# Block 3's state projection by Strassen's scheme among the output products, the residual seeded into Z, and one sum of block 0 and two S4 sums by DMA

## The chip, the cores and the metric

One core of a Trainium2 chip. The metric is device time in microseconds (us), the median of several executions. The traces below are of one execution each; a trace's span is about 2 us shorter than the time. A ratio is the mean time of one kernel's fast runs over that of the other's of the same rounds on the same chip, so it is not quite the ratio of the medians that are quoted.

Names used below: PE is TensorE's matmuls (PEld its weight loads), DVE is VectorE, ACT is ScalarE, POOL is GpSimd, SP is SyncE, which here only issues DMAs. PSUM is the memory in which matmuls leave their results; to evacuate it is to copy them out. An accumulating DMA adds what it carries to what stands at its destination; its landing is the moment at which the transfer is complete. PEq and SPq in the views are the sequencers of PE and SP. "L504" is line 504 of the kernel that ran, so one statement has different numbers in different kernels.

## The reference

The input is x of shape (1, 2048, 512). It is layer-normalised, and three things are added: x itself, a diagonal state-space model, and a gated MLP.

```python
xn = _layernorm(x)                                  # (x - mean) / sqrt(var + 1e-5)
# state-space part, complex, 512 states
Bu   = einsum("bld,pd->blp", xn, B_bar)             # "state projection": re and im parts
h_t  = Lam_bar * h_{t-1} + Bu_t                     # a scan over 2048 steps
y    = 2 * einsum("blp,dp->bld", h, Cmat).real + xn * Dskip
# gated MLP, 1792 hidden units
out2 = (silu(xn @ w1) * (xn @ w3)) @ w2
return x + y + out2                                 # bfloat16
```

## The kernel before

The 2048 rows are cut into four blocks (0 to 3) of 512. Each block has these stages: the MLP's first two products ("gate stage", `glu`), the state projection (`bu`), a chain of VectorE and DMA steps around the scan (`ssm_tasks`), and the output products (`y_fast`). Rows of the output are done in eight pairs of 128-row tiles: pairs 0 and 1 belong to block 0, pairs 2 and 3 to block 1, pairs 4 and 5 to block 2, pairs 6 and 7 to block 3. Each pair is a 2 x 2 block product by the Winograd form of Strassen's scheme: seven products instead of eight, for sums of the factors (S1 to S4 of the left one, T1 to T4 of the right one). The gate stage of block 3 uses the same scheme (`glu_last`), so the kernel already knows how.

The order of TensorE's work in the second half is: gate stage of block 2, projection of block 3, pairs 2 and 3, gate stage of block 3, pairs 4 to 7.

VectorE's work is queued in a list (`bg`, class `Filler`) and taken out while TensorE works, with an estimate of both engines' clocks. All of it is fixed when the kernel is built; in the traces a piece of VectorE's work keeps its place in that order even when its operands are ready sooner (in e3, below, a 0.4 us addition with its operand ready at 176.6 us started at 183.14, behind 6 us of other work).

```python
class Filler:                                    # shortened
    def fill(self, lead=None):                   # emit queued work while the VectorE clock is behind
        limit = self.pe + (self.lead if lead is None else lead)
        while self.tasks and self.dve + 0.5 * self.tasks[0][0] <= limit:
            if not getattr(self.tasks[0][1], "ready", lambda: True)():
                return
            self.pop()
    def flush(self, key):                        # emit everything up to the last task with this key
        last = max((i for i, t in enumerate(self.tasks) if t[2] == key), default=-1)
        for _ in range(last + 1):
            self.pop()
```

```python
def bu(b):                                       # state projection: 32 matmuls of 512 columns
    for hf in range(NPT // 2):
        u = up.tile([P, 2, 2, TBLK], BF16, name="u")
        for j in range(2):
            for ri in range(2):
                ...
                for dt in range(NDT):
                    nc.tensor.matmul(out=ps, lhsT=bt[:, ri, dt, ...], rhs=xnT_blk[b][:, dt, :], ...)
                nc.scalar.activation(out=u[:, j, ri, :], in_=ps, func=ACT.Copy)

def ssm_tasks(b, posts_last=False, between=(), middle=(), late=()):
    def half(hf):                                # two halves of the states
        def pre_c():                             # u += p : on VectorE for block 0 and half 0 of block 2
            if b == 0 or (b, hf) == (2, 0):
                nc.vector.tensor_tensor(out=st["g"], in0=st["g"], in1=st["p"], op=ALU.add)
            else:
                gp.dma_start(out=st["g"], in_=st["p"], accum_op=ALU.add)   # an accumulating DMA
        def scan(j, ri): ...                     # 4 scans of 1.2 us in each half
        def post_c():                            # act += p16: by accumulating DMA, but for the last half
            ...
    if b == 0:
        add(*pre0, *scans0, *post0, *pre1, *scans1, *post1)
        return
    ...

def row_sums(n, b, p):                           # S3 = a11-a21, S1 = a21+a22, S2 = a22-S3
    return [S3 on VectorE,
            S1 on VectorE if n in (0, 1, 6, 7) else S1 by accumulating DMA,
            S2 on VectorE]                       # (in words; the code is in the whole kernel)

def y_fast(n, then=()):                          # output products of pair n, shortened
    def product2():
        mms(f, v["a12"], weight(1, D1), False)
        nc.vector.tensor_tensor(out=v["s4"], in0=v["a12"], in1=v["s2"], op=ALU.subtract)   # S4
        add(o1[:, D1], f, o1[:, D1])
        if n + 1 < len(pairs) and n not in (1, 3):
            seeds(n + 1)                         # residual of the next pair into PSUM; flushes ("res", b)
    def product7():
        mms(g, v["s3"], tsum[2], False)
        add(q[2], g, o2[:, D1])                  # three PSUM additions
        add(o2[:, D2], g, q[1])
        add(o2[:, D1], z, q[2])
        store(c1 + 1, o2)
    ...
    for i in ((1, 5, 2, 6, 4, 3, 7) if b == 0 else (1, 4, 2, 6, 5, 7, 3)):
        products[i - 1]()
```

## Time and profile before

Median 203.0 us (202.85 to 203.09). What matters:

| stage | from, us | PE busy | DVE busy |
|---|---|---|---|
| start, gate stage and scan of block 0 | 0 to 50 | 49.2 of 50 | 42.9 |
| blocks 1 and 2 | 50 to 117 | 66.8 of 67 | 66.1 |
| projection of block 3, pairs 2 and 3 | 117 to 141 | 24.0 of 24 | 22.1 |
| gate stage of block 3 | 141 to 164 | 23.0 of 23 | 22.1 |
| pairs 4 and 5 | 164 to 181 | 17.0 of 17 | 15.2 |
| pairs 6 and 7 | 181 to 198 | 17.0 of 17 | 11.5 |

Five of the lines behind it, from the view of busy time by stretches of the kernel before; the first is the second part of block 0. The columns are: stretch, its length, busy time (and instructions) of PE, PEld, DVE, ACT and POOL, granted clock of TensorE as a share, mean load of the DMA engines, GB/s.

```profile
35.00:50.00 15.00, 15.00 (x71) 6.86 (x70) 14.90 (x17) 13.22 (x24) 3.62 (x4) 1.00 0.66 194
...
117.00:141.00 24.00, 24.00 (x188) 18.17 (x187) 22.06 (x30) 7.94 (x16) 6.56 (x5) 1.00 0.66 98
141.00:164.00 23.00, 23.00 (x152) 14.62 (x150) 22.07 (x32) 17.54 (x33) 0.86 (x1) 1.00 0.42 68
164.00:181.00 17.00, 17.00 (x156) 15.05 (x154) 15.24 (x24) 3.29 (x9) 2.84 (x2) 1.00 0.50 68
181.00:198.00 17.00, 17.00 (x179) 15.48 (x177) 11.46 (x23) 2.15 (x7) 0.00 (x0) 1.00 0.11 37
```

TensorE is busy all the time. A busy PE need not be a fast one, so the pace has to be read too: in the chain of waits, 8 matmuls of 512 columns take 1.73 us and 22 of 256 columns take 2.40 us, 216 and 109 ns each. These are three lines of the kernel before's chain (start, length, what):

```profile
117.72 1.73 PE bu_ps L438 x8
...
133.04 2.40 PE y_ps L865 x22
...
141.44 3.45 PE gu_ps L671 x16
...
```

From the first to the last of these, 141.44 - 117.72 = 23.72 us, TensorE did block 3's projection and pairs 2 and 3. And these are all the waits of TensorE that the waits view of the kernel before shows (engine, line, for whom: us in total, times, longest):

```profile
PE bu_ps L194 <- PEq L1049: 0.8, 1, 0.8
PE gu_ps L539 <- DMA xnT<-xn: 0.2, 1, 0.2
```

So the kernel's time is the sum of its TensorE work, a head of 5 us and a tail of 3 us. VectorE has little room: in 35 to 117 us it is busy 99% of the time.

### The profile page before, as it was taken

To read this page: it belongs to the slowest core of one execution; us is meant where nothing else is said; L and a number is where in the kernel's file an instruction comes from. 1 tells how busy PE (TensorE), PEld (TensorE's weight loads), DVE (VectorE), ACT (ScalarE), POOL (GpSimd) and SP (SyncE) were. 2 spreads that over 40 slices of the span, in tenths; PEclk is the share of its full clock that TensorE was granted. 3 is DMA by queue.
4 is the path that set the end of the run, shared out by engine and by line. 5 is a ranking of instruction groups with operands and counts; after the bars stand their busy time and mean duration, and the time that the engine had idled before them with its cause. 6 is when DMAs were issued, how large, how long until landed. Compare 5 with 4: busy or idle time off the path is not lost.

```text
span 201.1 us, 3551 instructions
## 1 busy us (share of the span) xinstructions
PE 197.2 (98%) x1353; PEld 126.4 (63%) x1353; DVE 180.4 (90%) x256; ACT 127.2 (63%) x257; POOL 47.9 (24%) x70
## 2 busy tenths in 40 slices
PE   8999999999999999999999999999999999999994
PEld 2974444444444588844444445888566678888893
DVE  4699699999999999989999989998989998988833
ACT  4799788699999967957797676110588771101110
POOL 7160289600310053043005011315100003100000
PEclk9999999999999999999999999999999999999999
DMA  5999995980582043925895955294960002951011
GB/s 160 328 248 258 290 157 170 347 216 0 105 156 55 0 91 68 177 87 106 132 157 104 97 106 108 17 156 80 163 148 0 3 0 15 113 104 52 10 62 39
DMA packets 34225, 23.56 MB, mean 117 GB/s; under 512 B 21792, under 2 KB 32160, under 8 KB 34208
## 3 DMA queue, kind: packets, MB, share of 16 engines
q0 software_dynamic: 8096, 9.84, 32.3%
q1 hardware_dynamic: 25536, 13.21, 26.6%
q10 hardware_dynamic: 576, 0.30, 0.5%
q8 instruction: 10, 0.16, 0.3%
q14 instruction: 7, 0.06, 0.1%
HBM read 7.74 MB, written 2.10 MB: 49 GB/s over the span
## 4 chain that ended last, share of the span: by engine, by line
PE 59%; DVE 33%; DMA 3%; issue 2%; POOL 1%; ACT 1%; DVEq 0%
PE gu_ps L865 13%; PE gu_ps L539 12%; PE y_ps L865 7%; PE gu_ps L671 7%; PE bu_ps L865 4%; DVE u L484 4%; DVE act L557 4%; PE y_ps L438 3%; PE bu_ps L438 3%; PE y_ps L693 3%; DMA xnT<-xn 3%; DVE tw L796 2%; PE bu_ps L194 2%; DVE u L467 2%; DVE p L463 2%
## 5 line engine op out<-in xcount | busy, mean ns | idle before, releaser
L539 PE MATMUL gu_ps<-xnT,w_sb 128*128 128x512 bf16 x312 | 68.2, 379 | 0.2 <-DMA xnT<-xn 0.2
L539 PEld LDWEIGHTS <-w_sb 128*128 128x128 bf16 x312 | 30.4, 98 | 36.8 <-DMA xnT<-xn 0.5
L865 PEld LDWEIGHTS <-act 128*128 128x128 f16 x462 | 43.5, 98 | 5.4
L549 ACT ACTIVATE u<-gu_ps 128x512 bf16<-128x512 f32 x41 | 24.8, 606 | 5.8 <-PE gu_ps L539 5.1
L548 ACT ACTIVATE g<-gu_ps 128x512 bf16<-128x512 f32 x41 | 24.7, 603 | 5.4 <-PE gu_ps L539 5.1
L438 PEld LDWEIGHTS <-bt 128*128 128x128 bf16 x128 | 12.5, 98 | 15.1
L484 DVE TENSOR_TENSOR_SCAN u<-rho,act,u 128x512 bf16<-128x512 f32 x16 | 19.8, 1269 | 0.0
L824 POOL DMA_DIRECT2D act<-act x4 | 8.0, 2002 | 33.8 <-DVE tw L820 28.9
L865 PE MATMUL gu_ps<-w_sb,act 128*128 128x256 bf16 (+3 forms) x126 | 15.9, 267 | 0.0
L671 PE MATMUL gu_ps<-xnT,w_sb 128*128 128x512 bf16 x64 | 15.9, 379 | 0.0
L438 PE MATMUL y_ps<-xnT,bt 128*128 128x512 bf16 x64 | 15.1, 379 | 0.0
L438 PE MATMUL bu_ps<-xnT,bt 128*128 128x512 bf16 x64 | 15.1, 379 | 0.0
L557 DVE TENSOR_TENSOR act<-g,u 128x1024 f16<-128x1024 bf16 x21 | 14.2, 678 | 0.6 <-ACT u L549 0.6
L501 POOL DMA_DIRECT2D act<-p x7 | 6.3, 907 | 32.2 <-DVE act L494 28.2
L683 ACT ACTIVATE g<-gu_ps 128x512 bf16<-128x512 f32 x14 | 8.4, 598 | 5.7 <-PE gu_ps L671 5.3
L440 ACT ACTIVATE u<-y_ps 128x512 bf16<-128x512 f32 x16 | 9.5, 595 | 2.3 <-PE y_ps L438 2.1
L440 ACT ACTIVATE u<-bu_ps 128x512 bf16<-128x512 f32 x16 | 9.5, 595 | 2.0 <-PE bu_ps L438 1.9
L865 PE MATMUL bu_ps<-w_sb,act 128*128 128x256 bf16 (+3 forms) x84 | 10.4, 264 | 0.0
L865 PE MATMUL gu_ps<-ct,act 128*128 128x256 f16 (+1 forms) x72 | 10.4, 267 | 0.0
L484 DVE TENSOR_TENSOR_SCAN u<-rho,ends,u 128x512 bf16<-128x512 f32 x8 | 10.0, 1271 | 0.0
L467 DVE TENSOR_TENSOR u<-u,tabe 128x2048 bf16<-128x2048 bf16 x8 | 9.8, 1220 | 0.1
L490 DVE TENSOR_TENSOR p<-u,tabe 128x2048 f16<-128x2048 bf16 x8 | 9.8, 1220 | 0.1
(163 smaller groups left out, 342.3 us busy)
## 6 DMA issues: line engine op xcount, KB each, us to landing
act<-p POOLq DMA_DIRECT2D x7, 512.0 KB, 5.2
xn<-x_blk POOLq DMA_DIRECT2D x4, 512.0 KB, 5.8
out_dram<-xn SPq DMA_DIRECT2D x15, 128.0 KB, 2.6
w_sb<-in_B_w_dram SPq DMA_DIRECT2D x1, 1792.0 KB, 8.0
w_sb<-in_B_w_dram SPq DMA_DIRECT2D x2, 768.0 KB, 5.9
u<-x_blk POOLq DMA_DIRECT2D x3, 512.0 KB, 6.5
act<-act POOLq DMA_DIRECT2D x4, 352.0 KB, 6.8
w_sb<-in_B_w_dram SPq DMA_DIRECT2D x4, 256.0 KB, 4.3
```

The costliest lines, as they stand in the source:

```text
L438: nc.tensor.matmul(out=ps, lhsT=bt[:, ri, dt, pt * P:(pt + 1) * P], rhs=xnT_blk[b][:, dt, :], start=(dt == 0), stop=(dt == NDT - 1))
L440: nc.scalar.activation(out=u[:, j, ri, :], in_=ps, func=ACT.Copy)
L467: nc.vector.tensor_tensor(out=st["g"], in0=st["g"], in1=tabe[:, psl, 0:1, :].to_broadcast(FULL), op=ALU.mult)
L484: nc.vector.tensor_tensor_scan(out=v, data0=rho[:, pt:pt + 1].to_broadcast([P, TBLK]), data1=v, initial=init, op0=ALU.mult, op1=ALU.add)
L490: nc.vector.tensor_tensor(out=st["p16"][:, :, ::-1, :], in0=st["g"], in1=tabe[:, psl, 1:3, :], op=ALU.mult)
L539: nc.tensor.matmul(out=ps[:, tsl], lhsT=w[:, dt, f * P:(f + 1) * P], rhs=xnT[:, dt, tsl], start=(dt == 0), stop=(dt == NDT - 1))
L548: nc.scalar.activation(out=g16[:, f % 2, :], in_=g_ps, func=ACT.Silu)
L549: nc.scalar.activation(out=u16[:, f % 2, :], in_=u_ps, func=ACT.Copy)
L557: nc.vector.tensor_tensor(out=act(b)[:, k0:k1 + 1:k1 - k0, :], in0=g16, in1=u16, op=ALU.mult)
L671: nc.tensor.matmul(out=ps, lhsT=w[:, dt, f * P:(f + 1) * P], rhs=xnT[:, dt, :], start=(dt == 0), stop=(dt == NDT - 1))
L683: nc.scalar.activation(out=g16[:, f % 2, :], in_=side(w1_sb, f), func=ACT.Silu)
L865: nc.tensor.matmul(out=out, lhsT=left[:, k, :], rhs=right[k][:, cols], start=(start and k == 0), stop=(k == NK - 1), skip_group_check=True)
```

## The change

The intent is to take columns off TensorE. Block 3's projection is done by Strassen's scheme too: seven products of 4 matmuls of 256 columns for each half, 56 in all, instead of 32 of 512. To give the scheme's sums and PSUM evacuations time, the seven steps are woven between the products of pairs 2 (half 0) and 3 (half 1). That costs VectorE some 5 us, which is given back elsewhere: the residual is seeded into the PSUM tile Z, so product 7 needs two PSUM additions instead of three; S4 of pairs 4 and 5 is formed by an accumulating DMA and the third product, which needs it, is put off into the next pair; and one of the sums of block 0's states goes from VectorE to an accumulating DMA.

The core of the diff (renamings, moved sums, signs and the new function's inner steps are cut):

```diff
+    LATER = (4, 5)
@@ ssm_tasks
             def pre_c():
-                if b == 0 or (b, hf) == (2, 0):
+                if (b, hf) in ((0, 0), (2, 0)):
                     nc.vector.tensor_tensor(out=st["g"], in0=st["g"], in1=st["p"], op=ALU.add)
                 else:
                     gp.dma_start(out=st["g"], in_=st["p"], accum_op=ALU.add)
@@
         if b == 0:
-            add(*pre0, *scans0, *post0, *pre1, *scans1, *post1)
+            add(*pre0, *pre1, *scans0, *post0, *scans1, *post1)
@@ new: bu_fast(b, hf), the Strassen projection of one half
+        def one():
+            product(g, a11, b11, True)
+            copy(f, g)
+            subtract(s2, s13, a11)
+        ...
+        return deque(((one, five), (two, six), (seven,), (three,), (four,)))
@@ y_fast
+        nc.scalar.activation(out=z, in_=o2[:, D1], func=ACT.Copy)     # in seeds(): residual into Z
...
-            bg.own(0.85, -1.1)
-            nc.vector.tensor_tensor(out=v["s4"], in0=v["a12"], in1=v["s2"], op=ALU.subtract)
+            if n in LATER:
+                gp.dma_start(out=v["s4"], in_=v["s2"], accum_op=ALU.add)
+            else:
+                bg.own(0.85, -1.1)
+                nc.vector.tensor_tensor(out=v["s4"], in0=v["a12"], in1=v["s2"], op=ALU.add)
...
-            mms(z, v["a22"], tsum[3], True)
+            mms(z, v["a22"], tsum[3], False)
+            copy(q[2], z)
...
-            add(q[2], g, o2[:, D1])
+            add(o2[:, D1], g, q[2])
             add(o2[:, D2], g, q[1])
-            add(o2[:, D1], z, q[2])
@@ the loop over the products
-            products[i - 1]()
+            if i == 3 and n in LATER:
+                later[n] = product3
+            else:
+                products[i - 1]()
+            if i == 5 and n - 1 in later:
+                later.pop(n - 1)()
+                if n + 1 < len(pairs):
+                    seeds(n + 1)
+            if between:
+                for step in between.popleft():
+                    step()
+                    bg.fill()
@@ the main sequence
-    bu(3)
-    posts = ssm_tasks(3, True, between=up_sums(3))
-    res_difference(3)
-    posts()
-    y_fast(2, row_sums(3, *pairs[3]))
-    bg.flush(("ssm", 2))
-    y_fast(3, row_sums(4, *pairs[4]))
+    bg.flush("cols")
+    ssm_tasks(3, middle=[(0.0, after_y2, None), *row_sums(4, *pairs[4])])
+    res_difference(3)
+    keep_ends(1)
+    y_fast(2, row_sums(3, *pairs[3]), bu_fast(3, 0))
+    y_done.append(2)
+    y_fast(3, (), bu_fast(3, 1))
```

## The prediction

> **What bounds the kernel now.** TensorE. In the table of busy time by stage, PE is busy from about 5 to 198 us but for one gap of 0.2 us near 86 (a wait for the transposed block 2); the span is 201.1 us. It also runs at full pace: in the chain of waits 8 matmuls of 512 columns take 1.73 us (216 ns each), 11 of 256 columns 1.20 us (109 ns each), and the granted clock is 1.00. [...] So time falls only if PE gets fewer columns. VectorE is a close second: 180 us busy, 96 to 99% from 25 to 118, 93% from 118 to 190 (66.6 of 72 us).
>
> **What the change removes.** Block 3's projection is 6.91 us of PE (four pieces of 1.73 in the chain). Strassen makes it 56 matmuls of 256 columns: at 109 ns, 6.1 us. Gain on PE: 0.8 us. All else on PE keeps its count.
>
> **What it adds and moves on VectorE.** New: two halves x (three sums at about 0.34 us start to start, two PSUM adds at 0.64) and two first sums, about 5.3 us. Given back: one PSUM add of 0.34 us in each of eight pairs by seeding the residual into Z (2.7), S4 of pairs 4 and 5 (2 x 0.81), one 1.14 us add of block 0 sent by DMA: about 5.4. Net near zero; the column sums only move earlier. ScalarE gains two 0.37 us copies per pair, in windows where it is 1 to 2 us busy of 8.
>
> So the critical path loses 0.8 us, if VectorE keeps its dates. That is the risk: block 3's u comes later relative to its scans (half 0 at the end of pair 2, half 1 late in pair 3), so more is left to do between 140 and 181. From start-to-start durations I get about 37 us of VectorE work in some 40 before pair 6 needs block 3's states. Today pair 6's S2 ends at 184.3, about 0.3 us before its product; the reordered S2 wins back 0.8. The accumulating DMAs of this shape landed after 6.6 to 7.7 us; S4 of pair 4 has about 9 us between issue and its deferred product, S1 of pair 5 about 7. I allow 0.2 us of PE stalls.
>
> The tail (last PE end 198.2, last VectorE add 198.5, last store to 201.1) should stay: the last adds wait for the last product's halves, not for the removed add. The head should stay too.
>
> **Predicted: 202.4 us** (203.0 - 0.8 + 0.2), 8 in 10 between 201.7 and 203.5. Faster by over 2%: 0.01; within 2%: 0.975; slower by over 2%: 0.015.
>
> **What would show it right.** PE busy without new gaps; block 3's projection as 14 products of 0.44 us among pairs 2 and 3; the last gate stage (141.3 us) starting about 0.8 us earlier; VectorE busy 180 +/- 1.5 us; the tail unchanged.
>
> **What would show it wrong.** PE gaps in pairs 2 and 3 that wait for VectorE (column sums come only just before pair 2); PE gaps in pairs 5 and 6 that wait for VectorE or an accumulating DMA; pair 4 (164.5) not starting earlier. With several such gaps the time could be 204 to 206. If freed VectorE time instead closes the gap near 86: 202.0.

"Full pace" rests on the granted clock of 1.00. 203.0 - 0.8 + 0.2 = 202.4 us, with 0.8 from the measured 216 and 109 ns (6.91 - 6.1) and 0.2 the author's estimate.

## The result, and the profile after

The changed kernel takes 207.92 us (207.55 to 208.36, 4 runs) against 203.01 us for the kernel before; the ratio is 1.0244, with a 95% interval of 1.0218 to 1.0269. It is slower by 2.4%, outside the predicted range.

First the same view of stretches, for the changed kernel. The stages begin later here, so the borders from 117 us on are moved with them (121, 144, 167, 185).

```profile
35.00:50.00 15.00, 12.20 (x58) 5.58 (x57) 10.57 (x13) 9.14 (x17) 2.79 (x4) 1.00 0.86 225
...
121.00:144.00 23.00, 23.00 (x212) 20.50 (x210) 21.31 (x34) 10.78 (x24) 3.69 (x3) 1.00 0.43 63
144.00:167.00 23.00, 22.84 (x146) 14.30 (x148) 22.24 (x28) 17.62 (x33) 3.73 (x4) 1.00 0.62 96
167.00:185.00 18.00, 16.65 (x151) 14.55 (x150) 16.03 (x21) 4.87 (x14) 6.74 (x4) 1.00 0.87 86
185.00:203.00 18.00, 17.71 (x183) 15.80 (x181) 11.74 (x22) 3.12 (x10) 0.00 (x0) 1.00 0.27 54
```

The stretch of 121 to 144 us shows the intended effect, and it is exactly as large as intended. In the chain of waits of the changed kernel these lines mark its ends:

```profile
121.27 1.20 PE gu_ps L965 x11
...
144.19 0.21 PE gu_ps L764
...
```

144.19 - 121.27 = 22.92 us for the projection and pairs 2 and 3 together, 0.80 us less than the 23.72 of before. TensorE is busy all of it. The loss lies elsewhere, and the waits of TensorE name it. All of them, for the changed kernel:

```profile
PE gu_ps L544 <- ACT g L553: 2.8, 1, 2.8
PE gu_ps L965 <- DMA act<-x_blk: 1.4, 1, 1.4
PE bu_ps L965 <- DVE act L1007: 0.9, 1, 0.9
PE bu_ps L195 <- PEq L1174: 0.8, 1, 0.8
PE gu_ps L965 <- DMA act<-p: 0.3, 1, 0.3
```

Four gaps are new: 2.8 us near 48 us, 0.9 near 79, 1.4 near 182 and 0.3 near 185. That is 5.4 us, less the 0.2 us gap of before that is gone, less the 0.8 us gained: 4.4 us of the 4.8 by which the spans differ (205.9 and 201.1).

### The gap near 48 us

The releaser that the waits view gives, ACT, is only the last link. Here is the timeline of the changed kernel around it, PE, DVE, ACT, POOL and SP mixed and lines left out (start, length, engine, line, operation, out<-in, and in brackets how long the engine was idle before it, and for whom):

```profile
31.21 0.57 SPq L182 DMA_DIRECT2D w_sb<-in_B_w_dram  x1
...
31.80 1.25 DVE L470 TENSOR_TENSOR u<-u,tabe 128x2048 bf16<-128x2048 bf16 x1
...
35.92 1.00 POOL L477 DMA_DIRECT2D u<-p  x1
...
39.78 1.21 DVE L497 TENSOR_TENSOR act<-u,tabe 128x2048 f16<-128x2048 bf16 x1
...
45.41 1.22 DVE L487 TENSOR_TENSOR_SCAN u<-rho,u 128x512 bf16<-128x512 f32 x1 [4.43 <-DMA u<-p]
46.56 0.67 DVE L562 TENSOR_TENSOR act<-g,u 128x1024 f16<-128x1024 bf16 x1
...
47.31 0.60 ACT L553 ACTIVATE g<-gu_ps 128x512 bf16<-128x512 f32 x1 [4.14 <-DVE act L562]
...
47.96 2.32 PE L544 MATMUL gu_ps<-xnT,w_sb 128*128 128x512 bf16 x10 [2.80 <-ACT g L553]
```

Read backwards. TensorE starts again at 47.96, when ACT had emptied a PSUM tile. ACT had been waiting 4.14 us for a VectorE multiplication (L562), because it needed a buffer that this multiplication frees. That multiplication stands in VectorE's queue behind a scan (L487), and the scan waited 4.43 us for the accumulating DMA `u<-p`, the block 0 sum that used to be a VectorE addition. Its data were ready at 33.05, when L470 ended; it was issued at 35.92, after GpSimd's queue had worked off a row of small operations; and it landed at 45.4. In the kernel before, the same place reads:

```profile
41.10 1.22 DVE L472 TENSOR_TENSOR u<-u,p 128x2048 bf16<-128x2048 bf16 x1
...
42.25 0.68 DVE L557 TENSOR_TENSOR act<-g,u 128x1024 f16<-128x1024 bf16 x1
...
42.85 1.22 DVE L484 TENSOR_TENSOR_SCAN u<-rho,u 128x512 bf16<-128x512 f32 x1
```

The addition (L472) takes 1.2 us, and the multiplication and the scan follow at once. The landing times of these DMAs, from the view of the source line, are first those of the changed kernel (six transfers, `u<-p` and the like; the 9.5 is block 0's) and then those of the kernel before (five; the 8.7 is one issued at 138 us, 1.1 us behind another accumulating DMA):

```profile
DMA to landing us min/median/max: 4.5/5.0/9.5
```
```profile
DMA to landing us min/median/max: 4.6/5.6/8.7
```

### The gaps near 182 and 185 us

The third product of pair 4 was put off into pair 5 to give S4's DMA time, and it still came too early. From the timeline of the changed kernel, lines left out:

```profile
170.54 1.93 POOL L920 DMA_DIRECT2D act<-act  x1 [12.25 <-DVE tw L913]
...
171.62 2.80 POOL L1004 DMA_DIRECT2D act<-x_blk  x1
...
172.94 2.42 POOL L504 DMA_DIRECT2D act<-p  x1
...
181.98 0.94 PE L965 MATMUL gu_ps<-w_sb,act 128*128 128x256 bf16 x7 [1.35 <-DMA act<-x_blk]
...
185.61 0.61 PE L965 MATMUL gu_ps<-ct,act 128*128 128x256 f16 x4 [0.29 <-DMA act<-p]
```

Three accumulating DMAs are issued within 3 us: S1 of pair 5 (L920), S4 of pair 4 (L1004) and the states of block 3's first half (L504). S4 lands 10.3 us after its issue, and the states 12.6 us. The same kind of transfer (L920 here, L824 before, 352 KB in rows of 256 bytes; the trace of the kernel before has 1424 packets for the one at 167.65 us) landed after 6.6 to 7.7 us in the kernel before, which was the basis of the prediction. Two of those four had no other accumulating DMA issued near them (6.6 us each), and two had one of 512 KB issued within 1.1 us (7.7 and 6.9 us); none had a second one of its own kind just ahead:

```profile
DMA to landing us min/median/max: 10.3/10.3/10.3
```
```profile
DMA to landing us min/median/max: 6.6/6.8/7.7
```

### The profile page after: what moved, and what is told of

Its sections match the earlier page's. It is cut to its first block, busy times and chain, and to the rows that moved or that the text cites. A ratio compares the mean times of both kernels' runs of the same rounds, so it can differ in the third digit from the quotient of the medians.

```text
span 205.9 us, 3633 instructions
## 1 busy us (share of the span) xinstructions
PE 196.4 (95%) x1365; PEld 128.3 (62%) x1377; DVE 180.3 (88%) x258; ACT 133.2 (65%) x277; POOL 50.7 (25%) x73
## 4 chain that ended last, share of the span: by engine, by line
PE 47%; DVE 22%; issue 16%; DMA 9%; POOL 3%; ACT 1%; POOLq 0%; ACTq 0%; DVEq 0%
PE gu_ps L965 13%; PE gu_ps L544 12%; DMA act<-p 6%; PE y_ps L965 5%; PE bu_ps L965 4%; DMA xn<-x_blk 3%; DVE act L562 3%; PE bu_ps L195 2%; DVE u L470 2%; DVE p L466 2%; DVE u L487 2%; PE gu_ps L764 2%; PE y_ps L439 2%; PE bu_ps L439 2%; PE gu_ps L689 1%
## 5 line engine op out<-in xcount | busy, mean ns | idle before, releaser
L487 DVE TENSOR_TENSOR_SCAN u<-rho,ends,u 128x512 bf16<-128x512 f32 x16 | 19.8, 1269 | 0.0
L504 POOL DMA_DIRECT2D act<-p x7 | 7.7, 1103 | 39.0 <-DVE act L497 36.3
L439 PEld LDWEIGHTS <-bt 128*128 128x128 bf16 x96 | 9.4, 98 | 11.3
L562 DVE TENSOR_TENSOR act<-g,u 128x1024 f16<-128x1024 bf16 x21 | 14.1, 676 | 0.9 <-ACT u L554 0.9
L487 DVE TENSOR_TENSOR_SCAN u<-rho,u 128x512 bf16<-128x512 f32 x8 | 9.4, 1209 | 4.4 <-DMA u<-p 4.4
L920 POOL DMA_DIRECT2D act<-act x4 | 8.3, 2069 | 16.8 <-DVE tw L913 16.8
L439 PE MATMUL y_ps<-xnT,bt 128*128 128x512 bf16 x47 | 11.3, 379 | 0.1
L439 PE MATMUL bu_ps<-xnT,bt 128*128 128x512 bf16 x46 | 11.2, 379 | 0.1
L470 DVE TENSOR_TENSOR u<-u,tabe 128x2048 bf16<-128x2048 bf16 x8 | 9.8, 1226 | 0.2
L487 DVE TENSOR_TENSOR_SCAN u<-rho,act,u 128x512 bf16<-128x512 f32 x8 | 9.9, 1269 | 0.0
L497 DVE TENSOR_TENSOR act<-u,tabe 128x2048 f16<-128x2048 bf16 x8 | 9.7, 1217 | 0.0
```

The lines of the kernel that those rows point to most:

```text
L439: nc.tensor.matmul(out=ps, lhsT=bt[:, ri, dt, pt * P:(pt + 1) * P], rhs=xnT_blk[b][:, dt, :], start=(dt == 0), stop=(dt == NDT - 1))
L470: nc.vector.tensor_tensor(out=st["g"], in0=st["g"], in1=tabe[:, psl, 0:1, :].to_broadcast(FULL), op=ALU.mult)
L487: nc.vector.tensor_tensor_scan(out=v, data0=rho[:, pt:pt + 1].to_broadcast([P, TBLK]), data1=v, initial=init, op0=ALU.mult, op1=ALU.add)
L497: nc.vector.tensor_tensor(out=act_state(b, hf), in0=st["g"], in1=tabe[:, psl, 0:1, :].to_broadcast(FULL), op=ALU.mult)
L562: nc.vector.tensor_tensor(out=act(b)[:, k0:k1 + 1:k1 - k0, :], in0=g16, in1=u16, op=ALU.mult)
```

## The experiments

The theory at this point (A): the whole loss is two DMA landings, one in block 0 and one in pair 4; the gap near 79 follows from the first one. The rivals: the new order of VectorE's work in block 0 causes the first gap; or VectorE is too late for pairs 4 to 6 whatever the DMAs do (C). What is left of theory A there is that transfers under way together land later: in h1 block 0's DMA beside the loads, in g1 and w3 S4 of pair 4 among three accumulating DMAs issued within 5 us.

In the table, the gaps are what TensorE was idle in the profiled execution (us), from the waits and the timeline. "Half clock" says for how long the granted clock was 0.5 during or after a gap. It agrees within 0.2 us with an estimate from the mean granted clock of stretches, with the clock taken as 1.0 or 0.5 in them: w3 has 0.88 over 182 to 185.6 us, 0.50 to 190 and 0.80 to 194; e3 0.80 over 177 to 183.6 and 0.52 to 188; f1 0.69 over 186 to 190 and 0.89 to 194; e2 0.64 over 48.5 to 53.2, 0.78 over 181 to 190 and 0.85 to 200. Medians of the kernel before, on the chips used, were 203.0 to 203.2. Waits of 0.2 to 0.6 us within the first 8 us, which some of these traces have, are left out.

| kernel | us | ratio to before | near 48 | near 79 | pair 4's S4 | pair 5 | pair 6: states | pair 6: S2 | half clock |
|---|---|---|---|---|---|---|---|---|---|
| changed kernel | 207.92 | 1.0244 | 2.8 | 0.9 | 1.4 | | 0.3 | | |
| e1 block 0 sum on VectorE | 204.64 | 1.0079 | | | 1.4 | | 0.3 | 0.4 | |
| e2 S4 on VectorE | 212.45 | 1.0478 | 3.0 | | | 4.4 | | | 3.4 + 6.8 us |
| e3 both on VectorE | 210.03 | 1.0354 | | | | 5.8 | | | 6.8 us |
| e4 before, block 0 sum by DMA | 207.00 | 1.0192 | 2.8 | 0.9 | | | | | |
| f1 e3, other queue order | 207.90 | 1.0242 | | | | 0.2 | 3.4 | | 3.4 us |
| g1 e1, S1 of pair 5 on VectorE | 204.16 | 1.0066 | | | | | 1.2 | 0.9 | |
| h1 loads held back | 204.14 | 1.0060 | | | 1.4 | | 0.3 | | |
| j1 e1 without S4 (wrong sum) | 203.74 | 1.0032 | | | | | 0.4 | 0.9 | |
| w1 h1 + g1 + product moved | 203.64 | 1.0019 | | | | 1.3 | | | |
| w2 w1, block 0 as in e1 | 203.52 | 1.0019 | | | | 1.3 | | | |
| w3 w1, S1 of pair 5 by DMA | 208.57 | 1.0281 | | | 1.4 | 2.6 | 0.3 | | 6.8 us |
| w4 w1, product moved further | 202.06 | 0.9940 | | | | 0.1 | | | |

Under "pair 5" the wait is for a PSUM addition in e2 and e3, for S1 in f1 and for S4 in w1 to w4. All twelve experiments passed the comparison with the reference. (So did j1, whose S4 is wrong: probably the two wrong products weigh too little beside the residual for the comparison to see it.)

The clock has its own price, apart from the gaps. The four executions of f1 took 206.38 us at a mean granted clock of 1.000, 207.86 and 207.93 at 0.992, and 209.40 at 0.984: 1.5 us more at 0.992 (the execution of 207.86 us is the traced one, with 3.4 us at half clock) and 3.0 us more at 0.984. In e3, whose four executions all have 0.984, the trace has by estimate 4.2 us of matmuls at half clock (0.52 over 183.6 to 188 us, TensorE busy for 4.39 of the 4.4), so some 2 us of its time are clock. The traces of e2 and w3 are of their slowest executions (214.17 and 210.11 us, mean clock 0.976 and 0.984); the other three have 0.984 to 0.992.

### e1 and e4: block 0's sum

e1 is the changed kernel with the sum back on VectorE; the new order of block 0's steps stays.

```diff
-                if (b, hf) in ((0, 0), (2, 0)):
+                if b == 0 or (b, hf) == (2, 0):
...
-        transfers = ... + (pre1[2],) + ...
+        transfers = ... + ((pre1[2],) if b > 0 else ()) + ...
```

> The changed kernel with one part undone: the second sum of block 0 (its second state half) is again added on VectorE instead of by an accumulating DMA; the new order of block 0's steps stays. Theory A (the DMA's landing, 4.4 us of VectorE wait at 41 to 45 us, starves ScalarE and then TensorE): the 2.8 us gap of TensorE at 48 us disappears and, if the late S4 of pair 0 (0.9 us gap at 79) is its consequence, that one too; time 204.0 to 205.2. Rival B (the gap comes from VectorE having more to do in front of the gates, the new order of block 0): the VectorE wait goes but the gap stays at 1.5 us or more, time above 206.5.

Measured: 204.64 us, 3.3 less than the changed kernel, and both early gaps are gone. So the new order is innocent. The gap near 79 comes and goes with the one near 48 in the changed kernel, e1, e4 and h1, so it is most likely its consequence; e2 alone has the first without the second, and TensorE also lost time at half clock there (a mean of 0.64 over 48.5 to 53.2 us).

e4 puts only this part into the kernel before: the same order, the same DMA.

```diff
-                if b == 0 or (b, hf) == (2, 0):
+                if (b, hf) in ((0, 0), (2, 0)):
...
-        transfers = ... + ((pre1[2],) if b > 0 else ()) + ...
+        transfers = ... + (pre1[2],) + ...
...
-            add(*pre0, *scans0, *post0, *pre1, *scans1, *post1)
+            add(*pre0, *pre1, *scans0, *post0, *scans1, *post1)
```

> The kernel before with only this part of the change: block 0's two sets of steps before the scans in the new order, its second sum by an accumulating DMA. Theory A: the same wait of VectorE of about 4 us near 41 and the same TensorE gap of 2.5 to 3 us near 48, with a second gap near 79 to 86 if the kernel before has no slack there: 205.5 to 207.0. Rival B' (the gap needs the rest of the change): within 0.5 us of 203.0.

Measured: 207.00 us, 3.8 more than the kernel before (203.23 there), at the upper end of what A expected. Its waits of TensorE are those of the changed kernel's first half:

```profile
PE gu_ps L539 <- ACT g L548: 2.8, 1, 2.8
PE bu_ps L865 <- DVE act L904: 0.9, 1, 0.9
```

Undoing it alone and doing it alone agree: this one part is worth 3.3 to 3.8 us of the 4.9 us lost. (The profiled execution of e4 took 206.63 us at full clock, 3.4 us more than the kernel before; the other three, 206.99 to 207.29 us, have a mean clock of 0.990 or 0.991, so theirs was below full for a while.)

### h1: why that DMA landed late

Two things stood between the data and the landing: a late issue (2.9 us behind GpSimd's small operations) and a long transfer (9.5 us). Just ahead of it, from 31.2 us on, SP had issued a 1.8 MB weight load and five loads of x. h1 holds those back. A one-column write to the weight's tile on VectorE, placed behind block 0's first four scans, makes the load wait (it was issued at 38.41 instead of 31.21 us); the block 0 sum stays a DMA.

```diff
     def late_loads():
+        nc.vector.tensor_copy(out=w2_sb[:, 0, 0:1], in_=rstd_all[:, 0:1])
         nc.sync.dma_start(out=w2_sb, in_=B_w2...)
...
-    bg.add(0.0, late_loads, ("ln", 1))
...
-            add(*pre0, *pre1, *scans0, *post0, *scans1, *post1)
+            add(*pre0, *pre1, *scans0)
+            bg.add(0.1, late_loads, ("ssm", 0))
+            add(*post0, *scans1, *post1)
```

> The changed kernel, with the load of the 1.8 MB weight and of blocks 2 and 3 of x held back (by a one column write to the weight's tile on VectorE) until block 0's first scans are issued, at about 38 us instead of 31. Theory A1 (block 0's accumulating DMA lands after 9.5 us instead of 5 [...]): it lands within 6.5 us, VectorE waits 1.5 us or less for it, the 2.8 us gap goes; 204.0 to 205.3. Rival A2 (it is late because its issue waits behind GpSimd's small operations and the transfer is slow by itself): landing 8.5 us or more, 207 or more.

Measured: 204.14 us. The issue is as late as before (36.12), the landing is not. From the timeline and the source view of h1:

```profile
36.12 1.00 POOL L478 DMA_DIRECT2D u<-p  x1
...
38.41 0.37 SPq L183 DMA_DIRECT2D w_sb<-in_B_w_dram  x1
...
41.45 1.22 DVE L488 TENSOR_TENSOR_SCAN u<-rho,u 128x512 bf16<-128x512 f32 x1 [0.19 <-DMA u<-p]
```
```profile
DMA to landing us min/median/max: 4.5/5.0/5.4
```

The scan now waits 0.19 us instead of 4.43. So the transfer was slow because of the loads beside it, not by itself. (They were held back together; which of them matters was not tried.) The landing took 9.5 us with the loads issued from 4.7 us ahead of it, 5.3 us with them issued from 2.3 us behind it. The late issue alone did not hurt here, though it had used up the slack.

### e2, e3 and f1: S4 back on VectorE

e2 empties the list of pairs whose S4 is a DMA; e3 does that and e1 together.

```diff
-    LATER = (4, 5)
+    LATER = ()
```

> The changed kernel with one part undone: S4 of pairs 4 and 5 on VectorE and their third product in its old place (the list of deferred pairs is empty). Theory A (S4 of pair 4 lands 10 us after its issue, later than the 9 us it has, so the deferred product waits 1.4 us, and the next DMA lands late with it): both gaps near 182 and 186 go, time 206.0 to 206.8. Rival C (VectorE is simply too far behind in pairs 4 to 6, and S4 on it makes that worse): new waits of TensorE for VectorE of over 1 us in pairs 4 to 6, time 207.5 or more.

> Both parts undone at once: block 0's sum and S4 of pairs 4 and 5 on VectorE. What is left of the change is the Strassen projection, the residual seeded into Z and the moved sums. Theory A: all four gaps of TensorE go and the 0.8 us saved by the projection shows: 202.0 to 203.0, below the kernel before. Rival C: VectorE cannot carry it, gaps in pairs 4 to 6, 203.5 to 206.

Both expectations of theory A failed. e2 took 212.45 us and e3 210.03 us: the two late gaps are gone, and a larger one is in their place. e2 is in the range of rival C; e3 lies above even that rival's. The new wait of e3 is this one:

```profile
PE y_ps L965 <- DVE x_blk L976: 5.8, 1, 5.8
```

Product 7 of pair 5 waits 5.8 us for a PSUM addition (`x_blk`, L976) that frees its PSUM tile. The timeline of e3 shows why (PE and DVE, lines left out):

```profile
176.78 2.45 DVE L487 TENSOR_TENSOR_SCAN u<-rho,act,u 128x512 bf16<-128x512 f32 x2
...
181.66 1.23 DVE L502 TENSOR_TENSOR act<-act,p 128x2048 f16<-128x2048 f16 x1
182.80 0.42 DVE L860 TENSOR_TENSOR xn<-xn 128x512 f16<-128x512 bf16 x1
183.14 0.42 DVE L976 TENSOR_TENSOR x_blk<-y_ps,xn 128x256 f32<-128x256 f32 x1
183.61 2.51 PE L965 MATMUL y_ps<-tw 128*128 128x256 f16 x11 [5.82 <-DVE x_blk L976]
```

The addition (183.14) needs 0.4 us, and its operand had been ready since product 6 ended at about 176.6. It stands behind two scans and the whole end of block 3's state work (the last of it is L502). That is an order of emission: seeding pair 6 flushes everything up to block 3's residual difference (L860), which the change queues behind all of block 3's state work. The trace shows VectorE working through this in order: 6 us of scan and state work (176.78 to 182.8 us) with TensorE standing still for 5.8.

f1 is e3 with one line moved: the difference is queued ahead of the state work.

```diff
+    res_difference(3)
     ssm_tasks(3, middle=[(0.0, after_y2, None), *row_sums(4, *pairs[4])])
-    res_difference(3)
```

> The run with both parts back on VectorE, plus one move: block 3's residual difference is queued ahead of block 3's scan work instead of behind it. Seeding pair 6 forces everything up to that difference to be emitted, and in the run before that put 6 us of scan work in front of one 0.4 us PSUM add that product 7 of pair 5 waits for. Theory D (the order of VectorE's queue made the 5.8 us gap): that gap goes; what is left is VectorE's lateness, a wait of 2 to 3.5 us where pair 6 first needs block 3's states; 206 to 208. Theory E (VectorE's load alone makes it, the order does not matter): 209.5 to 210.5, with the same total of gaps.

Measured: 207.90 us (206.38 to 209.40), inside the range that theory D gave. The 5.8 us gap is gone; in its place TensorE waits 3.4 us where pair 6 first needs block 3's states:

```profile
PE gu_ps L965 <- DVE act L502: 3.4, 1, 3.4
```

So theory C is right in this: VectorE is late for pair 6. It ends the states (L502) at 186.1 in f1. Giving it S4's two operations of 0.8 us back, as e2, e3 and f1 do, makes that worse.

### g1 and j1: what the DMAs of pairs 4 and 5 cost

g1 starts from e1 and puts S1 of pair 5 on VectorE, so that only two accumulating DMAs remain near 167 to 173 us.

```diff
-        if n in (0, 1, 6, 7):
+        if n in (0, 1, 5, 6, 7):
             one = (0.9, ... S1 on VectorE ...)
```

> The changed kernel with block 0's sum on VectorE (204.6 measured), and also S1 of pair 5 on VectorE instead of by DMA. S4 of pair 4 landed 10.3 us after its issue there, behind S1 of pair 5 and beside the states' transfer. Theory A [...]: S4 of pair 4 now lands within 8 us, the gap of 1.4 us before its deferred product and the 0.3 us wait for the states' transfer go; one added VectorE operation of 0.8 us may move into pair 6; 203.0 to 204.2. Rival F (this transfer takes 10 us whatever is beside it): the gap stays above 1 us, 204.3 to 205.5.

Measured: 204.16 us. S4's DMAs landed after 6.7 us instead of 10.3, and the gap before the deferred product is gone, as A expected. (The states' transfer was issued 5.6 us after S4 here and 3.6 us after it in e1; w1 and w3 below compare S1 alone.) But the ratio to the kernel before only went from 1.0079 to 1.0066, because VectorE's lateness came out in its place:

```profile
PE gu_ps L965 <- DVE act L502: 1.2, 1, 1.2
PE gu_ps L965 <- DVE x_blk L913: 0.9, 1, 0.9
```

j1 starts from e1 and does not form S4 of pairs 4 and 5 at all. It shows what pair 6 looks like when S4 costs nobody anything.

```diff
             if n in LATER:
-                gp.dma_start(out=v["s4"], in_=v["s2"], accum_op=ALU.add)
+                pass
```

> Wrong result on purpose: the changed kernel with block 0's sum on VectorE, and S4 of pairs 4 and 5 not formed at all (the product takes the unsummed factor), so neither VectorE nor a DMA pays for it. Theory A (late transfers make the remaining gaps): the gap at the deferred product goes and the states' transfer lands in time; gaps of TensorE from 120 us on sum to under 0.8 us; 202.4 to 203.4. Rival C (VectorE is behind anyway in pairs 5 and 6): gaps of 1.5 us or more there remain, waiting for VectorE; 204 or more.

Measured: 203.74 us, between the two expectations. The transfers' gaps are gone; 1.3 us of waits for VectorE remain at pair 6 (0.4 for the states, 0.9 for S2). So both theories hold a part: late landings, and a VectorE that is about 1 us late for pair 6 even with S4 free.

### w1 to w4: meeting the dates

If the loss is nothing but dates, a kernel that meets them should show the 0.8 us. w1 joins h1 and g1, and moves the deferred third product of pair 5 from behind the fifth product of pair 6 to behind its first, so that TensorE has 1.2 us of other work while VectorE ends the states.

```diff
-            if i == 5 and n - 1 in later:
+            if i == (1 if n == 6 else 5) and n - 1 in later:
                 later.pop(n - 1)()
-                if n + 1 < len(pairs):
-                    seeds(n + 1)
+            if i == 5 and n - 1 in LATER:
+                seeds(n + 1)
```

> The changed kernel with three dates mended: the bulk loads held back until block 0's first scans (block 0's sum stays a DMA), S1 of pair 5 on VectorE, and the deferred third product of pair 5 run after the first product of pair 6 instead of after its fifth, so that TensorE has 1.2 us of other work while VectorE ends block 3's states. Theory A plus C (the whole loss is dates: one landing in block 0, one landing in pair 4, and a VectorE that is 1 to 2 us late for pair 6): gaps of TensorE after 120 us under 0.5 us in all, and the 0.8 us of the projection shows: 202.0 to 202.9, 0.3 to 0.5% below the kernel before. Rival G (something else still costs time, for example more work on TensorE than counted): 203.2 or more although the gaps are gone.

Measured: 203.64 us, above the expected range, and the reason is plain in its waits: the moved product now comes too early for its own S4, which landed 6.8 us after its issue.

```profile
PE bu_ps L968 <- DMA act<-tw: 1.3, 1, 1.3
```

Everything else after 120 us is without a gap. w2 is w1 with block 0 as in e1 (VectorE has 1.1 us more to do), and w3 is w1 with S1 of pair 5 by DMA again.

> As the run before, but with the loads in their old place and block 0's sum on VectorE, which puts 1.1 us of work back on VectorE. If VectorE's lateness is what is left (theory C), its wait at pair 6 comes back in part, 0.3 to 1.2 us more than in the run before: 202.4 to 203.5. If not (rival), both agree within 0.2 us.

w2 took 203.52 us, the same as w1. Theory C is not refuted by it: VectorE ended the states at 182.3 in w2 and at 181.1 in w1, 1.2 us apart, but both were hidden behind the landing of S4, so the time says nothing. The run was badly placed to tell them apart.

> As the first of these, but with S1 of pair 5 by DMA again. Theory A [...]: S4 of pair 4 lands after 10 us again, the 1.4 us gap before its product comes back, 1 to 1.8 us above the first run. Rival: VectorE is what counts, and with 0.8 us less on it this run is as fast or faster than the first.

w3 took 208.57 us. The landing of S4 of pair 4 is at 10.3 us again, against 6.9 us in w1, as A expected. The edits of w1 and w3 differ only in S1 of pair 5. In w1 the states' transfer came 2.8 us after S4 and did not hold it up, and in e1 it came 3.6 us after S4, which still took 10.3 us; so it is S1, issued 1.1 us ahead of S4, that costs it 3.4 us. (GpSimd was also busy with S4's issue for 2.8 us in w3 and 1.9 in w1, so up to 0.9 of the 3.4 may lie there and not in the transfer.) But the loss over w1 is 4.9 us, not the 1 to 1.8 expected. The delay runs on: S4 of pair 5 landed after 10.3 us as well, its product waited 2.6 us, and behind three gaps that began within 6 us the granted clock of the profiled execution fell to 0.5 for 6.8 us (a mean of 0.50 over 185.6 to 190 us), some 6.0 us of which were matmuls at half pace.

w4 moves the product by one more place, behind the second product of pair 6:

```diff
-            if i == (1 if n == 6 else 5) and n - 1 in later:
+            if i == (4 if n == 6 else 5) and n - 1 in later:
```

> As the mended kernel, but the deferred third product of pair 5 runs after the second product of pair 6 (the fourth of the scheme), not after its first. In the mended kernel the only gap left after 120 us was 1.3 us there: S4 of pair 5 landed 6.8 us after its issue, at 182.0, and TensorE came for it at 180.7. Theory A plus C: in the new place TensorE first waits 0.4 us or so for VectorE to end block 3's states (they ended at 181.1 in the mended kernel), the landing is in time, gaps sum to under 0.7 us, and the projection's 0.8 us shows: 202.4 to 203.0, 0.1 to 0.4% below the kernel before. Rival G (something that is not a gap costs 0.6 us or more): within 0.1% of the kernel before or above it although the gaps are under 0.7 us.

Measured: 202.06 us (201.88 to 202.36) against 203.04 (202.73 to 205.65); the ratio is 0.994, with a 95% interval of 0.9897 to 0.9983. Every run of w4 was faster than every run of the kernel before, and the time is a little better than expected. (The one run of 205.65 us pulls the ratio down; the medians alone give 0.995.) The waits of TensorE are down to the one at the start:

```profile
PE bu_ps L196 <- PEq L1176: 0.8, 1, 0.8
```

TensorE is idle for 0.1 us after that, where pair 5's third product comes for its S4. The 0.98 us between the medians is about the 0.80 us of the projection and the 0.2 us gap near 86 that is gone. Rival G (something that is no gap costs 0.6 us or more) is refuted for w4.

## Why the prediction was right or wrong

Right:

- *"Gain on PE: 0.8 us."* It was 0.80 us (23.72 to 22.92), and w4 turned it into time. TensorE is the bound; that reading held.
- *VectorE "net near zero", 180 +/- 1.5 us.* It was 180.4 us before and 180.3 us after.
- *"The tail ... should stay."* The last matmul starts 3.2 us before the end of the span in the kernel before (198.0 of 201.1) and 3.0 us before it in the changed one (202.9 of 205.9).
- The named risks, PE gaps in pairs 5 and 6 that wait for VectorE or an accumulating DMA, are where a third of the loss was.

Wrong:

- The step that failed first is in the list of what is given back: *"one 1.14 us add of block 0 sent by DMA"*, together with *"The head should stay too"*. The DMA was booked as a gain of 1.14 us for VectorE and its landing was not dated. VectorE needed the result 8 us after giving it up (33.0 to 41.0); issue and transfer took 12.4 us (2.9 waiting behind GpSimd's operations, 9.5 beside a 1.8 MB load). VectorE got 1.1 us and waited 4.4 us. e1, e4 and h1 show this part to be 3.3 to 3.8 us.
- *"S4 of pair 4 has about 9 us between issue and its deferred product"* was about right, but the landing was mis-sized: it was read from four transfers that ran alone or beside one of another kind (6.6 to 7.7 us), and the change itself puts S4 1.1 us behind S1, a transfer of its own kind. It measured 10.3 us, and 6.7 to 6.9 us in g1 and w1, where S1 was back on VectorE.
- *"I allow 0.2 us of PE stalls"* for VectorE's lateness was too little. About 37 us of work in some 40 us was counted as fitting, as if VectorE could fill every moment. In j1, the last gate stage started at 140.7 us and VectorE ended the states at 181.8: of these 41.2 us it was busy for 39.5 and idle for 1.7, mostly waiting for TensorE. So the work was mis-sized by about 2.5 us, and the waits came on top. j1 shows 1.3 us of waits at pair 6 with S4 free, and g1 2.1 us with 0.8 us more on VectorE.
- *"the last gate stage (141.3 us) starting about 0.8 us earlier"* was wrong: it started 2.7 us later (144.0), as block 0's loss had been carried along. Here the bound engine did not make up a gap at 48 us.

What stays open: the 1 us by which VectorE is late for pair 6 was not split into its parts (the later arrival of block 3's u, the scheme's extra sums, the order of its queue), and which work the count of 37 us missed is not on record. f1 shows that the order matters; how much the other two do was not tried. w4 does not remove this lateness; it gives TensorE other work meanwhile.

## What to carry to other kernels

When work is moved from a full engine to a DMA, date the landing (issue wait plus transfer, beside everything else that will be under way at that moment) against the first in-order instruction that needs it; the busy time saved says nothing about that (here VectorE was spared 1.1 us and waited 4.4). When two engines are both near full, as here, expect a removed piece of the bound engine's work to pay only after the dates of the other engine have been met again: of these kernels only w4, with no gap over 0.2 us after the start, showed the 0.8 us. Undoing one part alone and doing it alone in the old kernel is a cheap pair of runs that put two thirds of this loss in one line.

## What the runs show of gaps, the clock and transfers

- The length of one gap of TensorE does not tell here whether a slow clock follows. In the traces of the changed kernel and e4 a gap of 2.8 us near 48 was followed by none (mean granted clock 1.00 over 48 to 53 us in the changed kernel, and 1.00 over 0 to 118 us in e4), but three other executions of e4 have a mean clock of 0.990 or 0.991; in e2 a gap of 3.0 us at the same place went with 0.64 over 48.5 to 53.2 us; and in w3 gaps of 1.4, 0.3 and 2.6 us went with 6.8 us at half clock. What decides was not shown; no run set out to test it.
- What other transfers do to the landing of an accumulating one: 512 KB landed after 4.5 to 5.4 us in h1 (the six transfers into `u`), and after 9.5 us behind a 1.8 MB load and others in the changed kernel; 352 KB landed after 6.9 us with 512 KB issued 2.8 us behind it (w1), and after 10.3 us with another 352 KB issued 1.1 us ahead of it as well (w3).
- Accumulating transfers of 352 KB in rows of 256 bytes landed after 6.6 to 7.7 us in the kernel before, and those of the states, 512 KB in long rows, after 5.2 us in the median. In the stretch of one of each (167 to 174.4 and 174.9 to 181 us) the trace has 1424 packets of 0.36 MB and 144 packets of 0.52 MB in the queue of these transfers. The first kind also held GpSimd for 1.9 us (2.2 once), the second for 0.9 us. No run changed the row length alone, so the cause is not shown.
